# Attention output through DRAM in rows of 448, and a projection of eleven products a tile

## The chip, the cores and the metric

The kernel runs on one core of a Trainium2 chip. The metric is the device time of one execution in microseconds (us); the kernel before has a median of 1062.87 us over three runs (1061.26 to 1063.69). A core has five engines that work side by side, each through its own instructions in their order: TensorE (PE, products of matrices into the banks of PSUM), VectorE (DVE), ScalarE (ACT), GpSimd (POOL) and SyncE (SP), which here only issues DMA transfers.

## The reference

The input x has 2048 rows of 448. Two branches are computed from it and mixed with a gate:

```
g = sigmoid(sum(x * gate_w))
a = attention(x) @ wo        # 16 heads of 28, softmax over 2048 keys
b = gelu(layernorm(x) @ w1 + b1) @ w2 + b2
out = g * a + (1 - g) * b
```

Attention has q, k and v from one matrix of 448 x 1344; scores are q k' / sqrt(28), and each head's output of 28 columns is put beside the others to 448 columns, ahead of wo (448 x 448). All arithmetic is in fp32 accuracy.

## The kernel before

PE multiplies operands in the type float32r, which keeps fewer bits than fp32. So each fp32 operand is split into a rounded high part and a rest, and a product of two operands takes three products of PE: high x high, high x low, low x high.

The stages in order of time: q, k and v are computed and kept in DRAM (0 to about 130 us); the MLP branch runs, and beside it the row maxima of the scores (to about 530 us); its result, with b2 added, is stored in DRAM as `gbs`, 16 tiles of 128 rows. Then comes attention (to about 1020 us), and last the projection with wo and the mix with the gate.

Attention goes over batches `n` from 0 to 15: a group `g` of four heads (`n // 4`) and a chunk `c` of 512 queries (`n % 4`). Each batch has 16 rounds over 128 keys. A round makes twelve products for scores (`scores`, L585), two exponentials on ACT (L594, L598) and four products with v (`value_round`, L762), which add up in bank 7. The four heads stand in partitions 0, 32, 64 and 96 there: 28 rows of output, then one row with the sum of the exponentials (v has a column of ones), then three unused rows.

At the end of a batch `finish` copies bank 7 to `ob` on DVE (L740), POOL's queue takes the four rows of sums to a small tile `lt` (L741), DVE inverts them (L745), POOL's queue writes them to DRAM (`rls`, L746) and brings them back spread over 32 partitions a head (`rc`, L748), and POOL multiplies `ob` by `rc` and splits it into `oh[g][c]` and `ol[g][c]` (L752 to L754). These 32 tiles stay in SBUF, with their unused rows.

The projection (`project`, L768) has 16 tiles of 128 queries, four a chunk. A tile multiplies, for each of the four groups, the high output with the high and the low wo and the low output with the high wo: twelve products (L777) into one of six banks. ACT scales the tile's base `ga`, which was loaded from `gbs`, by 1 - g (L779), DVE adds g times the product (L782), and SP stores the sum to the output (L784). There are six base tiles; the load for tile `tt + 6` (L786) goes into the base that the store of tile `tt` has emptied.

The order is written out by hand: the instructions of each engine run as the program issues them. A planner's clock (`Clock`) advances by a fixed time for each product or round that is issued, and `clock.at(dt, fn)` issues what `fn` holds once that clock has passed `dt` more; `flush` issues all that is left. These due times set only the order: on the chip, an engine works through its list as fast as its waits allow. SP's list holds in attention the loads of q, k and v for later batches (L130, L691) and the small transfers of the row maxima (L302), in the projection the output stores and base loads. `split_q` and `split_k` (L312 to L322) split q and k on POOL.

The projection's tile 0 stands ahead of the last two value rounds, tiles 1 to 11 follow them, then comes `clock.flush()`, then tiles 12 to 15, which need the last chunk.

Of the kernel before, what the change touches and what calls it, by code (L numbers as in the profile page):

```python
# [8 lines left out]
F32 = mybir.dt.float32  # L9
F32R = mybir.dt.float32r  # L10
# [6 lines left out]
P = 128  # L17
S = 2048
D = 448
H = 16  # L20
DH = 28
F = 1792
NG = 4
CH = 512
NC = S // CH
# [46 lines left out]
def kernel(ctx: ExitStack, tc: tile.TileContext, xt, wqk, wv, wo, xk, w1, b1, w2, b2,  # L72
                          ident_d, sel_d, out):
    nc = tc.nc
    ctx.enter_context(tc.manual_schedule())
    clock = Clock()

    const = ctx.enter_context(tc.tile_pool(name="const", bufs=1))
    dram = ctx.enter_context(tc.tile_pool(name="dram", bufs=1, space=DRAM))
# [25 lines left out]
    lns = dram.tile([2 * NT, P], F32, name="lns")  # L105
    gbs = dram.tile([NT, P, D], F32, name="gbs")
    rls = dram.tile([NG * NC, 4, CH], F32, name="rls")

    kr = [kq.tile([P, S], F32R, name=f"kr{i}") for i in range(2)]
    qr = [kq.tile([P, CH], F32R, name=f"qr{i}") for i in range(4)]  # L110
# [13 lines left out]
    def bank(b, n=CH):  # L124
        return ps[:, b, :n]
# [298 lines left out]
    with tc.tile_pool(name="qx", bufs=1) as qx:  # L424
# [105 lines left out]
        at = 3.8  # L530
# [56 lines left out]
    def scores(u):  # L587
        n, k = batches[u]
        a = 3 * (u % 2)
        for which in range(3):  # L590
            for j in range(4):
                product(n, k, j, a + j if j < 3 else 6, which)
        held[u] = z = pz[u % len(pz)]
        nc.scalar.activation(z, bank(6), AF.Exp, scale=SCALE)  # L594

    def exponentials(u):
        a, z, t = 3 * (u % 2), held[u], pt[u % len(pt)]
        nc.scalar.activation(t, ps[:, a:a + 3], AF.Exp, scale=SCALE)  # L598
        held[u] = [t[:, 0], t[:, 1], t[:, 2], z]

    def gates():
        nc.scalar.activation(gate, zall, AF.Exp, scale=-1.0)
        nc.vector.tensor_scalar_add(gate, gate, 1.0)
        nc.vector.reciprocal(gate, gate)
        nc.vector.tensor_scalar(ngate, gate, -1.0, 1.0, op0=OP.mult, op1=OP.add)
# [96 lines left out]
    at = att.enter_context(tc.tile_pool(name="at", bufs=1, reuse_waits="tile"))  # L702
    pt += [at.tile([P, 3, CH], F32, name=f"pt{i}") for i in range(1, 5)]
    pz += [at.tile([P, CH], F32, name=f"pz{i}") for i in range(2, 5)]
    oh = [[at.tile([P, CH], F32R, name=f"oh{g}_{c}") for c in range(NC)] for g in range(NG)]
    ol = [[at.tile([P, CH], F32R, name=f"ol{g}_{c}") for c in range(NC)] for g in range(NG)]
    woh = at.tile([P, NG, D], F32R, name="woh")
    wol = at.tile([P, NG, D], F32R, name="wol")
    ob = at.tile([P, CH], F32, name="ob")
    rc = at.tile([P, CH], F32, name="rc")  # L710
    lt = at.tile([P, CH // 32], F32, name="lt")
    ga = [at.tile([P, D], F32, name=f"ga{i}") for i in range(4)]
    flat = mx.rearrange("p g j t k -> p (g j t k)")
    ga += [flat[:, i * D:i * D + D] for i in range(2)]

    def load_wo(g):
        r = ga[g]
        nc.sync.dma_start(r, wo[:, g])
        clock.at(6.0, split_wo, g, r)

    def split_wo(g, r):
        nc.gpsimd.tensor_copy(woh[:, g], r)
        nc.gpsimd.tensor_sub(wol[:, g], r, woh[:, g].bitcast(F32))

    def load_qr(n):
        g, c = divmod(n, NC)
# [9 lines left out]
        load_heads(k, D, g, slice(0, S))  # L736

    def finish(n):
        g, c = divmod(n, NC)
        nc.vector.tensor_copy(ob, bank(7))  # L740
        nc.gpsimd.dma_start(lt, ob[DH:P:32, :])  # L741
        clock.at(4.0, finish_sum, n, g, c)

    def finish_sum(n, g, c):
        nc.vector.reciprocal(lt, lt)  # L745
        nc.gpsimd.dma_start(rls[n].rearrange("j (a b) -> (j a) b", b=CH // 32), lt)  # L746
        for j in range(4):
            nc.gpsimd.dma_start(rc[32 * j:32 * j + 32], rls[n, j].partition_broadcast(32))  # L748
        clock.at(8.0, finish_split, g, c)

    def finish_split(g, c):
        nc.gpsimd.tensor_mul(ob, ob, rc)  # L752
        nc.gpsimd.tensor_copy(oh[g][c], ob)
        nc.gpsimd.tensor_sub(ol[g][c], ob, oh[g][c].bitcast(F32))  # L754

    def value_round():
        u = state["round"]
        state["round"] += 1
        n, k = batches[u]
        t = held.pop(u)  # L760
        for j in range(4):
            nc.tensor.matmul(ps[32 * j:32 * j + 32, 7], vg[n // NC % 2][:, k, 32 * j:32 * j + 32],  # L762
                             t[j], start=(k == 0), stop=(k == NT - 1),
                             skip_group_check=True)
        if k == NT - 1:
            finish(n)

    def project(tt, b):  # L768
        c, i = divmod(tt, TPC)
        sl = slice(i * P, (i + 1) * P)  # L770
        g = ga[tt % 6]
        ops = []
        for h in range(NG):
            o, l = oh[h][c][:, sl], ol[h][c][:, sl]
            ops += [(o, woh[:, h]), (o, wol[:, h]), (l, woh[:, h])]
        for k, (w, x) in enumerate(ops):
            nc.tensor.matmul(bank(b, D), w, x, start=(k == 0), stop=(k == len(ops) - 1))  # L777
            clock.tick(MN)
        nc.scalar.activation(g, g, AF.Copy, scale=ngate[:, tt:tt + 1])  # L779
        halves = [(nc.sync, slice(0, D))] if tt < NT - 1 else [(nc.sync, slice(0, D // 2)), (nc.scalar, slice(D // 2, D))]  # L780
        for queue, s in halves:
            nc.vector.scalar_tensor_tensor(g[:, s], ps[:, b, s], gate[:, tt:tt + 1], g[:, s],  # L782
                                           op0=OP.mult, op1=OP.add)
            queue.dma_start(out[tt][:, s], g[:, s])  # L784
        if tt + 6 < NT:
            clock.at(4.0, lambda: nc.sync.dma_start(g, gbs[tt + 6]))  # L786

    for u, (n, k) in enumerate(batches):
        if k == 0:
            g, c = divmod(n, NC)  # L790
            if n > 0 and n + 3 < NG * NC:
                clock.at(3.0, load_qr, n + 3)
            if n + 2 < NG * NC:
                clock.at(1.0, split_q, n + 2)
            if c == 1 and g + 1 < NG:
                if g > 0:
                    clock.at(0.0, load_kr, g + 1)
                clock.at(8.0, load_v, g + 1)
            if c == 3 and g + 1 < NG:
                clock.at(2.0, split_k, g + 1)  # L800
            if n == 2:
                for h in range(NG):
                    load_wo(h)
            if n == 14:
                for tt in range(6):
                    nc.sync.dma_start(ga[tt], gbs[tt])
        if u > 1:
            scores(u)
        if u > 0:
            exponentials(u)  # L810
        if u == 8:
            gates()
        clock.tick(0.98)
        if u >= 2:
            value_round()
        clock.tick(0.87)
    project(0, 0)
    value_round()
    value_round()
    for tt in range(1, 12):  # L820
        project(tt, tt % 6)
    clock.flush()
    for tt in range(12, NT):
        project(tt, tt % 6)
    att.close()
# [53 lines left out]
```

## Time and profile before

| | us |
|---|---|
| median of three runs | 1062.87 |
| the profiled execution | 1064.28 |
| its span, first to last instruction | 1062.4 |
| PE busy | 1054.6 (99%) |
| ACT busy | 878.1 (83%) |
| DVE busy | 425.4 (40%) |
| POOL busy | 397.8 (37%) |
| first product of the projection | 1017.34 |
| share of the projection's line in the chain that ended last | 4% |

A row of the timelines reads: start, duration, engine, line, operation, what it writes and reads with shapes, how many were merged, and in brackets how long the engine sat idle before it and what ended that. A name followed by q (SPq) is an engine's issuing of a transfer. A row of the windows reads: the stretch, its length, then the busy time of PE, the weight loads, DVE, ACT and POOL with counts, the granted clock of TensorE as a share of full speed, the busy share of the DMA engines and GB/s. A row of the groups reads: line, engine, operation, shapes, count, then the busy time and the mean ns of one, then idle time before them with its releasers. A row of the chain reads: start, length, engine, line, count. Durations of products overlap, since they are pipelined; the distance of their starts is what counts.

### The profile page before, as it was taken

Reading aid. Unit: us, or ns where it says so; the run is one execution under the profiler, and the core shown is the slowest. Engines: PE = TensorE matmul, PEld = TensorE weight load, DVE = VectorE, ACT = ScalarE, POOL = GpSimd, SP = SyncE. Lnnn points to the kernel's source line nnn. Section 1 sums busy time; section 2 is a strip of 40 time slices with the busy share of each in tenths; the row PEclk is TensorE's granted clock in tenths of the full one; section 3 lists DMA queues with packets and bytes.
Section 4 is the critical chain, followed back from the end, with each engine's and each line's share of the span. In section 5 each row is a group of like instructions: output and inputs, shape, how many; then the busy total and the mean of one; then the engine's idle time right before and its main releaser. Section 6 shows DMA issues by size and latency. Waiting matters only on the chain.

```text
span 1062.4 us, 21453 instructions
## 1 busy us (share of the span) xinstructions
PE 1054.6 (99%) x8120; PEld 583.2 (55%) x8120; DVE 425.4 (40%) x1172; ACT 878.1 (83%) x1239; POOL 397.8 (37%) x410
## 2 busy tenths in 40 slices
PE   8999999999999999999999999999999999999998
PEld 6766766776677677766833333333333333333367
DVE  5488877887788778777300000000000000000012
ACT  5587789877875876686399999999999999999951
POOL 4354737652362336234213552323433242222211
PEclk9999999999999999999999999999999999999999
DMA  8798876513540551241003000300012002000024
GB/s 260 236 301 275 298 263 230 171 49 117 168 133 32 170 171 38 79 140 50 19 10 96 21 21 11 95 20 18 16 39 76 21 11 73 12 12 12 12 82 156
DMA packets 59088, 106.63 MB, mean 100 GB/s; under 512 B 11864, under 2 KB 31576, under 8 KB 58424
## 3 DMA queue, kind: packets, MB, share of 16 engines
q1 hardware_dynamic: 52696, 91.84, 27.8%
q0 software_dynamic: 5856, 12.78, 4.0%
q8 instruction: 64, 1.05, 0.4%
q10 hardware_dynamic: 432, 0.64, 0.2%
q14 instruction: 40, 0.33, 0.1%
HBM read 77.51 MB, written 26.64 MB: 98 GB/s over the span
## 4 chain that ended last, share of the span: by engine, by line
PE 97%; DMA 1%; ACT 1%; DVE 0%; issue 0%; POOL 0%; DVEq 0%; ACTq 0%
PE ps L336 38%; PE ps L762 24%; PE ps L585 22%; PE ps L176 6%; PE ps L777 4%; PE ps L171 4%; DMA kr<-qc 1%; DMA xraw<-in_xt 0%; POOL kr L505 0%; DVE wl L458 0%; ACT rl L258 0%; DVE xl L470 0%; ACT L688 0%; DVE rl L266 0%; ACT hf L328 0%
## 5 line engine op out<-in xcount | busy, mean ns | idle before, releaser
L258 ACT ACTIVATE rl<-ps 128x512 f32<-128x512 f32 x444 | 233.1, 598 | 81.8 <-PE ps L171 57.6
L598 ACT ACTIVATE pt<-ps 128x1536 f32<-128x1536 f32 x204 | 295.4, 1448 | 0.0
L266 DVE CUSTOM_DVE_ANT_0 rl<-rl,ps 128x512 f32<-128x512 f32 x444 | 280.7, 681 | 12.9 <-ACT rl L258 12.5
L762 PE MATMUL ps<-pz,vg 128*32 128x512 f32 x512 | 267.5, 605 | 0.0
L762 PE MATMUL ps<-pt,vg 128*32 128x512 f32 x1224 | 216.1, 605 | 0.0
L585 PEld LDWEIGHTS ps<-qh,kh 29*128 29x128 f32 x1024 | 49.3, 182 | 212.9 <-ACT pz L594 201.1
L740 DVE COPY ob<-ps 128x512 f32<-128x512 f32 x16 | 11.1, 692 | 383.4 <-PE ps L762 383.4
L594 ACT ACTIVATE pz<-ps 128x512 f32<-128x512 f32 x256 | 153.0, 598 | 7.9 <-PE ps L585 7.2
L336 PE MATMUL ps<-yh,w1t 128*128 128x512 f32 x448 | 136.6, 405 | 0.0
L181 DVE TENSOR_REDUCE mx<-ps 128x1 f32<-128x512 f32 x136 | 93.3, 688 | 96.5 <-PE ps L171 55.1
L585 PE MATMUL ps<-qh,kh 29*128 29x512 f32 x1024 | 129.9, 496 | 0.0
L637 POOL TENSOR_TENSOR hl<-hf,hh 128x512 fp32r<-128x512 f32 x56 | 72.2, 1289 | 118.2 <-ACT hh L328 114.9
L171 PE MATMUL ps<-kr,qr 28*128 28x512 f32 x570 | 104.1, 423 | 0.6 <-ACT zall L328 0.5
L585 PE MATMUL ps<-qr,kh 28*128 28x512 f32 x1024 | 104.5, 394 | 0.0
L585 PE MATMUL ps<-qh,kr 28*128 28x512 f32 x1024 | 104.1, 391 | 0.0
L336 PEld LDWEIGHTS ps<-yh,w1t 128*128 128x128 f32 x448 | 80.1, 188 | 33.5 <-issue 19.0
L336 PE MATMUL ps<-w2l,hh 128*128 128x448 f32 x224 | 85.0, 379 | 0.0
L336 PE MATMUL ps<-w2h,hl 128*128 128x448 f32 x224 | 84.7, 378 | 0.0
L336 PE MATMUL ps<-w2h,hh 128*128 128x448 f32 x224 | 84.2, 376 | 0.0
L176 PE MATMUL ps<-kd,qr 28*128 28x512 f32 x444 | 76.5, 497 | 0.0
L598 ACT ACTIVATE rl<-ps 128x1536 f32<-128x1536 f32 x52 | 75.3, 1448 | 0.0
L762 PEld LDWEIGHTS ps<-pt,vg 128*32 128x32 f32 x1224 | 30.8, 108 | 75.5 <-issue 70.6
(125 smaller groups left out, 1487.8 us busy)
## 6 DMA issues: line engine op xcount, KB each, us to landing
w1t<-w1s SPq DMA_DIRECT2D x56, 512.0 KB
qk<-qc SPq DMA_DIRECT2D x28, 256.0 KB
w1s<-w1t POOLq DMA_DIRECT2D x14, 512.0 KB, 5.2
qr<-qk SPq DMA_DIRECT2D x112, 56.0 KB
xr<-in_xt SPq DMA_DIRECT2D x18, 256.0 KB
kr<-qk SPq DMA_DIRECT2D x20, 224.0 KB
vs<-xraw SPq DMA_DIRECT2D x16, 256.0 KB
vg<-vs SPq DMA_DIRECT2D x4, 1024.0 KB
```

Source lines behind the costliest of these rows:

```text
L171: nc.tensor.matmul(bank(b), qr[self.qbuf[g, c]][r, i * P:(i + 1) * P], k[r, kb * CH:(kb + 1) * CH], start=True, stop=True)
L176: nc.tensor.matmul(bank(b), qr[self.qbuf[g, c]][r, i * P:(i + 1) * P], kd[g % 2][r, p], start=True, stop=True)
L181: nc.vector.reduce_max(mx[:, g, j:j + 1, c * TPC + i, kb], ps[:, b:b + 1], axis=AX)
L258: nc.scalar.activation(rl[:, b], bank(1 + b), AF.Relu)
L266: nc.vector.tensor_tensor_reduce(rl[:, b], rl[:, b], bank(k), 1.0, LOW, op0=OP.add, op1=OP.max, accum_out=mx[:, g, j, c * TPC + i, 2 * p:2 ...
L336: nc.tensor.matmul(bank(b, n), w, x, start=(i == 0), stop=(i == len(ops) - 1))
L585: nc.tensor.matmul(bank(b), w, x, start=(which == 0), stop=(which == 2))
L594: nc.scalar.activation(z, bank(6), AF.Exp, scale=SCALE)
L598: nc.scalar.activation(t, ps[:, a:a + 3], AF.Exp, scale=SCALE)
L637: nc.gpsimd.tensor_sub(hl[f], h, hh[f].bitcast(F32))
L762: nc.tensor.matmul(ps[32 * j:32 * j + 32, 7], vg[n // NC % 2][:, k, 32 * j:32 * j + 32], t[j], start=(k == 0), stop=(k == NT - 1), skip_gr ...
L777: nc.tensor.matmul(bank(b, D), w, x, start=(k == 0), stop=(k == len(ops) - 1))
```

## The change

The output of attention goes to a DRAM tensor `od` of 448 x 2048, without the unused rows, and is loaded back by chunks of 512 queries into four blocks of 128 partitions. 448 rows are three and a half blocks: the last 64 rows are loaded twice, into both halves of the fourth block, whose upper half then becomes the low part. So the fourth block needs two products in place of three, and a tile has 3 x 3 + 2 = 11. `wo` is loaded in the same order of rows, its last 64 rows twice, in 22 pieces.

The operands of a chunk are split by three DVE instructions (`split_o`): a copy of 128 x 2048, a subtraction of 128 x 1536 and one of 64 x 512. Two chunks' worth of tiles are kept, so a chunk takes the tiles of the one two before. Chunks 0 and 1 are loaded and split during the last two batches; chunk 2 is loaded after the last value round and split after tile 3; chunk 3 is loaded once its last group is stored, and split after tile 11.

The transfers of `lt`, `rls` and `rc`, which POOL's queue issued, are issued by SP, and so are the four stores to `od` of each batch. POOL keeps the multiplication alone. The due times of the last batch are shorter (2.5 and 5.0 in place of 4.0 and 8.0).

```diff
+    od = dram.tile([D, S], F32, name="od")
...
-    oh = [[at.tile([P, CH], F32R, name=f"oh{g}_{c}") for c in range(NC)] for g in range(NG)]
-    ol = [[at.tile([P, CH], F32R, name=f"ol{g}_{c}") for c in range(NC)] for g in range(NG)]
+    oraw = [at.tile([P, 4, CH], F32, name=f"oraw{i}") for i in range(2)]
+    oh = [at.tile([P, 4, CH], F32R, name=f"oh{i}") for i in range(2)]
+    ol = [at.tile([P, 3, CH], F32R, name=f"ol{i}") for i in range(2)]
...
+    def load_wo():
+        for h in range(H):
+            g, j = divmod(h, 4)
+            a, e = h * DH, h * DH + DH
+            cuts = [a] + [x for x in (P, 2 * P, 3 * P) if a < x < e] + [e]
+            for a, e in zip(cuts, cuts[1:]):
+                r = 32 * j + a - h * DH
+                for p in (a % P,) if a < 3 * P else (a % P, a % P + 64):
+                    nc.sync.dma_start(oraw[1][p:p + e - a, a // P, :D], wo[r:r + e - a, g])
+        clock.at(14.0, split_wo, 0)
...
+    def load_o(c):
+        cs, r = slice(c * CH, (c + 1) * CH), oraw[c % 2]
+        nc.sync.dma_start(r[:, 0:3], od[0:3 * P, cs].rearrange("(t p) n -> p t n", p=P))
+        for p in (0, 64):
+            nc.sync.dma_start(r[p:p + 64, 3], od[3 * P:D, cs])
+
+    def split_o(c):
+        r, h = oraw[c % 2], oh[c % 2]
+        nc.vector.tensor_copy(h, r)
+        nc.vector.tensor_sub(ol[c % 2], r[:, 0:3], h[:, 0:3].bitcast(F32))
+        nc.vector.tensor_sub(h[64:128, 3], r[64:128, 3], h[64:128, 3].bitcast(F32))
...
     def finish(n):
-        g, c = divmod(n, NC)
+        quick = n == NG * NC - 1
         nc.vector.tensor_copy(ob, bank(7))
-        nc.gpsimd.dma_start(lt, ob[DH:P:32, :])
-        clock.at(4.0, finish_sum, n, g, c)
+        nc.sync.dma_start(lt, ob[DH:P:32, :])
+        clock.at(2.5 if quick else 4.0, finish_sum, n, 5.0 if quick else 8.0)
+
+    def finish_sum(n, wait):
+        nc.vector.reciprocal(lt, lt)
+        nc.sync.dma_start(rls[n].rearrange("j (a b) -> (j a) b", b=CH // 32), lt)
+        for j in range(4):
+            nc.sync.dma_start(rc[32 * j:32 * j + 32], rls[n, j].partition_broadcast(32))
+        clock.at(wait, finish_store, n)
+
+    def finish_store(n):
+        g, c = divmod(n, NC)
+        nc.gpsimd.tensor_mul(ob, ob, rc)
         for j in range(4):
+            r = (4 * g + j) * DH
+            nc.sync.dma_start(od[r:r + DH, c * CH:(c + 1) * CH], ob[32 * j:32 * j + DH])
+        if n == NG * NC - 1:
+            load_o(3)
...
+        for t in range(4):
+            o = oh[c % 2][:, t, sl]
+            ops += [(o, woh[:, t]), (o, wol[:, t])]
+            if t < 3:
+                ops += [(ol[c % 2][:, t, sl], woh[:, t])]
...
+            if n >= 14:
+                clock.at(12.0 if n == 14 else 4.0, load_o, n - 14)
+                clock.at(20.0 if n == 14 else 14.0, split_o, n - 14)
...
     value_round()
     value_round()
+    load_o(2)
     for tt in range(1, 12):
         project(tt, tt % 6)
+        if tt == 3:
+            split_o(2)
     clock.flush()
+    split_o(3)
     for tt in range(12, NT):
         project(tt, tt % 6)
```

More of the change, by code (lines that the diff above doesn't have):

```diff
@@ L704 @@
     pz += [at.tile([P, CH], F32, name=f"pz{i}") for i in range(2, 5)]
-    oh = [[at.tile([P, CH], F32R, name=f"oh{g}_{c}") for c in range(NC)] for g in range(NG)]
-    ol = [[at.tile([P, CH], F32R, name=f"ol{g}_{c}") for c in range(NC)] for g in range(NG)]
-    woh = at.tile([P, NG, D], F32R, name="woh")
-    wol = at.tile([P, NG, D], F32R, name="wol")
+    oraw = [at.tile([P, 4, CH], F32, name=f"oraw{i}") for i in range(2)]
+    oh = [at.tile([P, 4, CH], F32R, name=f"oh{i}") for i in range(2)]
+    ol = [at.tile([P, 3, CH], F32R, name=f"ol{i}") for i in range(2)]
+    woh = at.tile([P, 4, D], F32R, name="woh")
+    wol = at.tile([P, 4, D], F32R, name="wol")
     ob = at.tile([P, CH], F32, name="ob")
@@ L714, with split_wo @@
     ga += [flat[:, i * D:i * D + D] for i in range(2)]
[L716 to L723, printed above, removed]
+    def load_wo():
[8 more added lines that the diff above has]
+        clock.at(14.0, split_wo, 0)
+    def split_wo(t):
+        r = oraw[1][:, t, :D]
+        nc.gpsimd.tensor_copy(woh[:, t], r)
+        nc.gpsimd.tensor_sub(wol[:, t], r, woh[:, t].bitcast(F32))
+        if t < 3:
+            clock.at(4.0, split_wo, t + 1)
+    def load_o(c):
[8 more added lines that the diff above has]
+        nc.vector.tensor_sub(h[64:128, 3], r[64:128, 3], h[64:128, 3].bitcast(F32))
     def load_qr(n):
@@ L738, in finish @@
     def finish(n):
-        g, c = divmod(n, NC)
-        nc.vector.tensor_copy(ob, bank(7))
-        nc.gpsimd.dma_start(lt, ob[DH:P:32, :])
-        clock.at(4.0, finish_sum, n, g, c)
-    def finish_sum(n, g, c):
-        nc.vector.reciprocal(lt, lt)
-        nc.gpsimd.dma_start(rls[n].rearrange("j (a b) -> (j a) b", b=CH // 32), lt)
-        for j in range(4):
[L748 to L754, printed above, removed]
+        quick = n == NG * NC - 1
+        nc.vector.tensor_copy(ob, bank(7))
+        nc.sync.dma_start(lt, ob[DH:P:32, :])
[7 more added lines that the diff above has]
+    def finish_store(n):
+        g, c = divmod(n, NC)
+        nc.gpsimd.tensor_mul(ob, ob, rc)
+        for j in range(4):
+            r = (4 * g + j) * DH
+            nc.sync.dma_start(od[r:r + DH, c * CH:(c + 1) * CH], ob[32 * j:32 * j + DH])
+        if n == NG * NC - 1:
+            load_o(3)
     def value_round():
@@ L772, in project @@
         ops = []
-        for h in range(NG):
-            o, l = oh[h][c][:, sl], ol[h][c][:, sl]
-            ops += [(o, woh[:, h]), (o, wol[:, h]), (l, woh[:, h])]
+        for t in range(4):
+            o = oh[c % 2][:, t, sl]
+            ops += [(o, woh[:, t]), (o, wol[:, t])]
+            if t < 3:
+                ops += [(ol[c % 2][:, t, sl], woh[:, t])]
         for k, (w, x) in enumerate(ops):
@@ L801 @@
             if n == 2:
-                for h in range(NG):
-                    load_wo(h)
+                load_wo()
+            if n >= 14:
+                clock.at(12.0 if n == 14 else 4.0, load_o, n - 14)
+                clock.at(20.0 if n == 14 else 14.0, split_o, n - 14)
             if n == 14:
```

## The prediction

> **What bounds the kernel now.** I read the busy table first, then the windows of the attention stretch, then the chain of work that ended last, and last the timelines of the tail engine by engine.
>
> ```profile
> PE 1054.6 (99%) x8120; PEld 583.2 (55%) x8120; DVE 425.4 (40%) x1172; ACT 878.1 (83%) x1239; POOL 397.8 (37%) x410
> ```
>
> ```profile
> 956.20:982.70 26.50, 26.50 (x284) 9.22 (x280) 0.94 (x2) 26.49 (x28) 6.41 (x9) 1.00 0.05 12
> ```
>
> ```profile
> L594 ACT ACTIVATE pz<-ps 128x512 f32<-128x512 f32 x250 | 149.4, 598 | 0.8 <-ACT pt L598 0.5
> ```
>
> The window row gives, after its length, the busy time of PE, weight load, DVE, ACT and POOL, then the granted clock, the DMA share and GB/s. In attention ACT works 26.49 of 26.50 us and sat idle 0.8 us ahead of 250 of its exponentials; DVE works 0.94 and POOL 6.41. Whatever the change does there is free as long as ACT never waits. The tail is different:
>
> ```profile
> 1017.41 2.67 PE ps L777 x12
> ...
> 1021.93 36.68 PE ps L777 x180
> 1058.61 0.03 issue
> ...
> 1058.70 0.45 DVE ga L782
> ```
>
> The projection is a gapless run of PE products: 36.68 / 180 = 0.2038 us each, 2.445 us a tile of twelve, and the end follows the last one. So a product saved is worth 0.2038 us, and a wait of PE costs its full length.
>
> **The products (L777).** Sixteen go, one a tile: 16 x 0.2038 = 3.26 us, all on the path. A tile now takes 11 x 0.2038 = 2.242 us. That is the whole gain; the rest of the change is what it costs to have the operands ready.
>
> **The attention stretch: taken as nothing.** POOL loses a cast and a subtraction a chunk and three kinds of DMA issue. Two splits on DVE (chunks 0 and 1; about 4.2 us each, priced below) lie in windows where DVE works 0.94 of 26.5 us. On SP the transfer of the sums waits for DVE's copy of bank 7, and behind it stand the next loads of q; before, these went out as soon as PE had released the tile:
>
> ```profile
> 589.15 1.63 SPq L130 DMA_DIRECT2D qr<-qk x4
> ```
>
> ```profile
> 619.94 0.61 POOL L312 CAST qh<-qr 128x512 fp32r<-128x512 f32 x1 [7.81 <-PE ps L585]
> ```
>
> A load going out at 589 is wanted by POOL's split no earlier than 620, so a delay of the five or six us by which the copy trails the start of a chunk is covered. Without that cover, each would hold ACT by what is missing. The output stores wait for POOL's multiplication, and behind them again stand only prefetches; the 22 pieces of wo (four before) have from chunk 2 to 1017. If a split stood ahead of the copy of bank 7, PE could wait 4.2 us at most; the splits are called 8 us or more away from it.
>
> **The tail, step by step.** Tile 0 is shorter by one product, so what follows moves 0.20 us ahead: tile 1 starts at 1021.66, tile k ends at 1021.66 + 2.242 k, that is tile 3 at 1028.4 and tile 11 at 1046.3. Tiles 12 to 15 read chunk 3, split by three DVE instructions that the program issues behind tile 11's. DVE takes its instructions in order:
>
> ```profile
> 1021.86 0.47 PE L777 MATMUL ps<-woh,oh 128*128 128x448 f32 x1
> ...
> 1048.51 0.36 PE L777 MATMUL ps<-woh,ol 128*128 128x448 f32 x1
> 1048.71 0.36 PE L777 MATMUL ps<-woh,oh 128*128 128x448 f32 x1
> ```
>
> ```profile
> 1022.06 0.69 DVE L740 COPY ob<-ps 128x512 f32<-128x512 f32 x1 [1.18 <-PE ps L762]
> 1024.64 0.68 DVE L782 SCALAR_TENSOR_TENSOR ga<-ps,gate,ga 128x448 f32<-128x448 f32 x1 [1.89 <-PE ps L777]
> 1028.70 0.25 DVE L745 RECIPROCAL lt<-lt 128x16 f32<-128x16 f32 x1 [3.37 <-DMA lt<-ob]
> 1028.87 1.33 DVE L782 SCALAR_TENSOR_TENSOR ga<-ps,gate,ga 128x448 f32<-128x448 f32 x2
> ...
> 1048.98 0.68 DVE L782 SCALAR_TENSOR_TENSOR mx<-ps,gate,mx 128x448 f32<-128x448 f32 x1 [1.75 <-PE ps L777]
> ```
>
> Tile 2 was through at 1021.86 + 2 x 2.445 = 1026.75, yet its sum ran at 1028.87, because the reciprocal ahead of it waited. So the split can't pass tile 11's sum, and that can't start before 0.27 us past tile 11 (1048.71 to 1048.98). Even with every transfer early, the split starts at 1046.3 + 0.27 + 0.68 = 1047.3, with PE idle since 1046.3.
>
> What the split costs, from DVE rows grouped by shape:
>
> ```profile
> L782 DVE SCALAR_TENSOR_TENSOR ga<-ps,gate,ga 128x448 f32<-128x448 f32 x11 | 7.5, 678 | 40.1 <-ACT ga L779 25.9 <-PE ps L777 14.1
> ...
> L470 DVE TENSOR_TENSOR xl<-xraw,xh 128x512 fp32r<-128x512 f32 x8 | 5.4, 689 | 4.5 <-ACT xh L328 4.5
> ...
> L121 DVE MEMSET kr<- 128x2048 f32 x1 | 1.8, 1765 | 0.4 <-issue 0.4
> ...
> L782 DVE SCALAR_TENSOR_TENSOR ga<-ps,gate,ga 128x224 f32<-128x224 f32 x2 | 0.8, 447 | 1.7 <-PE ps L777 1.7
> ```
>
> Slope (678 - 447) / 224 = 1.03 ns an element. Subtraction of 1536: 0.689 + 1024 x 1.03 ns = 1.74 us. No row shows a copy of 128x2048 on DVE: the memset of that shape took 1.77, the 0.69 copy extended at the slope gives 0.69 + 1536 x 1.03 ns = 2.27. I take 1.77, the row of the same engine and shape, and keep 2.27 for the range. Tile 12's first two products need only the copy; its third needs the long subtraction, which comes 1.74 - 0.41 = 1.3 us after they are done. The last subtraction (0.69) is over before tile 12 reaches its fourth block. So the split alone costs PE 0.95 (sum) + 1.77 + 0.15 (hand-over, an estimate from the 0.27 above) + 1.3 = 4.2 us.
>
> The Trainium skill, VectorE: DVE Perf Modes, section Mode 2×_2P, says that a copy with source and destination both in SBUF can run two fp32 elements a cycle, which would make this copy 1.2 us by an estimate and the sum 0.6 lower; no row here shows such a copy.
>
> **Whether the transfers are in time.** Prices:
>
> ```profile
> 684.21 0.46 SPq L691 DMA_DIRECT2D vg<-vs x1
> ```
>
> ```profile
> 686.00:687.00 1.00, 1.00 (x18) 0.28 (x12) 0.48 (x1) 1.00 (x2) 0.22 (x1) 1.00 0.95 281
> ...
> 689.00:690.00 1.00, 1.00 (x16) 0.50 (x12) 0.00 (x0) 1.00 (x2) 0.00 (x0) 1.00 0.32 68
> ```
>
> ```profile
> 1036.00:1037.00 1.00, 1.00 (x7) 0.93 (x6) 0.18 (x1) 0.44 (x1) 0.00 (x0) 1.00 0.80 303
> ```
>
> ```profile
> lt<-ob POOLq DMA_DIRECT2D x16, 8.0 KB, 3.1
> rls<-lt POOLq DMA_DIRECT2D x16, 8.0 KB, 1.7
> ```
>
> ```profile
> 996.57 1.99 POOL L748 DMA_DIRECT2D rc<-rls x4 [1.42 <-DMA rls<-lt]
> 1000.60 1.28 POOL L752 TENSOR_TENSOR ob<-ob,rc 128x512 f32<-128x512 f32 x1 [2.04 <-DMA rc<-rls]
> ...
> 1031.34 1.99 POOL L748 DMA_DIRECT2D rc<-rls x4 [1.52 <-DMA rls<-lt]
> 1037.50 1.29 POOL L752 TENSOR_TENSOR ob<-ob,rc 128x512 f32<-128x512 f32 x1 [4.17 <-DMA rc<-rls]
> ```
>
> ```profile
> 1033.40 0.33 SPq L786 DMA_DIRECT2D ga<-gbs x1
> ...
> 1042.82 0.38 SPq L786 DMA_DIRECT2D ga<-gbs x1
> ```
>
> ```profile
> 1037.87 0.67 ACT L779 ACTIVATE ga<-ga,ngate 128x448 f32<-128x448 f32 x1 [1.43 <-DMA ga<-gbs]
> ...
> 1045.38 0.67 ACT L779 ACTIVATE ga<-ga,ngate 128x448 f32<-128x448 f32 x1 [1.05 <-DMA ga<-gbs]
> ```
>
> A load of 1 MB moved its data until about 689.2, 5.0 us from its issue (load_o, three issues: 5.4). A 224 KB load took 2.56 us in a calm stretch and 4.47 in a crowded one, so a transfer waits for those ahead of it; at the 303 GB/s of a crowded microsecond of the old tail 224 KB hold the path 0.75. Issues cost about 0.35 each. The path of chunk 3:
>
> - DVE's copy ends at 1022.55; the sums' transfer goes at 1022.6 and lands at 1025.7 (3.1). Right behind it on SP is load_o(2), landed at 1028.4; its split follows tile 3's sum and is over by 1034, ahead of tile 8 (1037.3): free.
> - Reciprocal to 1025.95, rls issued at 1026.0. Landing after 1.7 would be 1027.7; behind load_o(2) and store 1 it is 1029.9. SP waits here with the four broadcasts, and behind them load 6, stores 2 and 3, load 7.
> - First broadcast to multiplication: 4.0, so 1033.9; 1.29 to 1035.2; four stores to od, issued by 1036.5, landed at 1038.2 (1.7). load_o(3) waits for that on SP, with load 8 and store 4 behind it; its data are in at 1043.6, still ahead of tile 11's end.
> - What is late next is the base of tiles 8 to 11 (ga). Load 8, store 4, load 9, store 5 follow the megabyte at 0.75 each: store 4 is through at 1045.1, store 5 at 1046.6. Load 11 refills the tile that store 5 empties: 1046.7 + 2.56 = 1049.3, ACT 0.67, DVE 0.68: the split of chunk 3, behind tile 11's sum, starts at 1050.7 in place of 1047.3.
>
> First product of tile 12: 1050.7 + 1.77 + 0.15 = 1052.6; PE has been idle 6.3 us.
>
> By the Trainium skill, DMA: Bandwidth & Descriptors, section Queues, rings and completion order, each engine takes one queue's descriptors in ring order, so moving the sums to the queue that carries megabytes puts 8 KB behind them: that speaks for the 6.3 and against the 2.9 of the first rival.
>
> **The clock** after such a pause:
>
> ```profile
> 492.00:493.00 1.00, 1.00 (x5) 0.90 (x5) 1.00 (x3) 0.15 (x1) 0.55 (x1) 0.89 1.17 326
> 493.00:494.00 1.00, 1.00 (x4) 0.91 (x3) 0.72 (x4) 0.00 (x0) 0.00 (x0) 0.50 1.25 298
> ...
> 496.00:497.00 1.00, 1.00 (x7) 0.79 (x5) 1.00 (x2) 1.00 (x3) 0.00 (x0) 0.90 0.00 0
> ```
>
> The one drop in this trace, after a thin stretch of PE, held half speed for about 3.4 us, which loses half of that: 1.7. A pause of 6.3 us should bring it; bounds 0 and 1.7, I take 1.7.
>
> **Sum:** -3.26 + 6.3 + 1.3 + 1.7 = +6.0 us. The profiled execution took 1064.28 us round a span of 1062.4, 1.4 above the median; the sum is a difference, so I set it on the median: 1062.87 + 6.0 = 1068.9, about **1069.0 us**.
>
> **Rivals.**
> - *The transfers are in time* (the other side). If small transfers pass the large ones and load 11 lands by 1045.9, only DVE's order is left: 0.95 + 1.77 + 0.15 = 2.9 us of idle, + 1.3 - 3.26 = +0.9, 1063.8 us, not told from no change. For it: the old tail, at up to 303 GB/s, had every base in time, and split chunk 3 on POOL right behind the multiplication at 1037.50, long before tile 12 at 1048.71. Against it: 4.47 against 2.56. If the clock still drops, +2.6: 1065.5.
> - *The transfers are worse.* The broadcasts took 6.2 us (1031.34 to 1037.50) in the crowded tail, and loads 4.47: + 2.2 + 1.9, and the copy at 2.27: +10.6, 1073.5 us.
> - *The split does not stand behind tile 11.* If DVE took it early, the 3.26 us remain: 1059.6. Against it stands the reciprocal's row.
>
> **How the numbers follow.** Forecast 0.60; in time 0.24, half with the clock kept; worse 0.12; early split 0.04. Less than 0.2% (2.1 us) can't be told from no change. Faster 0.04; same 0.14, the first rival with the clock kept and a little of its other half; slower 0.82. The range runs from the first rival, 1063.8, to the second, 1073.5.
>
> **What would show it.** Tiles of eleven products at 2.24 us; on DVE the 128x2048 copy behind tile 11's sum, PE idle by about 6 us at tile 12 with DVE as releaser, and a clock of 0.5 behind it; on SP broadcasts waiting for rls, load_o(3) for the stores of od, and ACT's scalings of bases 8 to 11 ending waits on DMA past 1044. Wrong would be a gap at tile 12 under 3.5 us (transfers in time), none, or waits of ACT in attention.

## The result, and the profile after

The changed kernel takes 1070.75 us (median of six runs, 1069.95 to 1072.54) against 1062.69 before on the same chip, 8.06 us more; the ratio is 1.0083, with a 95% interval of 1.0073 to 1.0093. 1069.0 had been predicted, in a range of 1063.8 to 1073.5.

The profiled execution after took 1070.4 us, that of before 1064.28. The one of before was slower than its six timed runs: its projection began at 1017.34, that of after at 1014.23, and its half clock at 492 to 497 us, which the prediction quotes, has no counterpart after. So the two tails are compared by their length, from the projection's first product to the end of the span: 1062.4 - 1017.34 = 45.06 us before, 1068.4 - 1014.23 = 54.17 after. The tail is 9.11 us longer, and the rest of the kernel is not slower.

PE in the tail, from the timeline of the kernel after (start, duration, what; in brackets the idle time before and its releaser):

```profile
1042.96 0.37 PE L806 MATMUL ps<-wol,oh 128*128 128x448 f32 x1
1051.85 0.74 PE L806 MATMUL ps<-woh,oh 128*128 128x448 f32 x1 [8.52 <-DVE oh L744]
1052.38 0.57 PE L806 MATMUL ps<-wol,oh 128*128 128x448 f32 x1
1053.64 0.74 PE L806 MATMUL ps<-woh,ol 128*128 128x448 f32 x1 [0.68 <-DVE ol L745]
...
1058.27 0.36 PE L806 MATMUL ps<-woh,oh 128*128 128x448 f32 x1
```

Tile 11's last product starts at 1042.96. The next could start 0.20 later; tile 12 starts at 1051.85, released by the copy of the split (L744). Its third product waits once more, for the long subtraction (L745). From there to 1058.27 are twelve steps at 0.386 us in place of 0.204.

What DVE did before that copy, from its timeline:

```profile
1036.06 0.68 DVE L811 SCALAR_TENSOR_TENSOR ga<-ps,gate,ga 128x448 f32<-128x448 f32 x1 [1.34 <-ACT ga L808]
1044.43 0.68 DVE L811 SCALAR_TENSOR_TENSOR ga<-ps,gate,ga 128x448 f32<-128x448 f32 x1 [7.69 <-ACT ga L808]
...
1049.97 0.69 DVE L811 SCALAR_TENSOR_TENSOR mx<-ps,gate,mx 128x448 f32<-128x448 f32 x1 [1.49 <-ACT mx L808]
1050.57 1.22 DVE L744 CAST oh<-oraw 128x2048 fp32r<-128x2048 f32 x1
1051.83 1.76 DVE L745 TENSOR_TENSOR ol<-oraw,oh 128x1536 fp32r<-128x1536 f32 x1
1053.62 0.69 DVE L746 TENSOR_TENSOR oh<-oraw,oh 64x512 fp32r<-64x512 f32 x1
```

The sum of tile 8 waited 7.69 us for ACT's scaling of its base and tile 11's ran at 1049.97; the split of chunk 3 stood behind it. Why the bases were late is on SP:

```profile
1022.46 0.43 SPq L769 DMA_DIRECT2D rls<-lt  x1
1028.57 1.71 SPq L771 DMA_DIRECT2D rc<-rls  x4
...
1033.64 1.61 SPq L779 DMA_DIRECT2D od<-ob  x4
1036.69 0.39 SPq L738 DMA_DIRECT2D oraw<-od  x1
...
1045.42 0.32 SPq L815 DMA_DIRECT2D mx<-gbs  x1
```

```profile
1049.27 0.67 ACT L808 ACTIVATE mx<-mx,ngate 128x448 f32<-128x448 f32 x1 [1.50 <-DMA mx<-gbs]
```

The 8 KB of the sums went out at 1022.46, and the broadcasts that wait for them at 1028.57: 6.1 us. The stores to od, load_o(3) and the base loads follow one after another; load 11 goes out at 1045.42 and ACT has it at 1049.27. In a calm stretch of attention the same pair on SP needs 1.55 us:

```profile
564.60 0.40 SPq L769 DMA_DIRECT2D rls<-lt  x1
566.15 1.71 SPq L771 DMA_DIRECT2D rc<-rls  x4
```

The clock, from the windows of PE in the kernel after (stretch, length, PE busy, granted clock, DMA share, GB/s):

```profile
1044.00:1048.00 4.00, 0.00 (x0) 1.00 0.72 187
1048.00:1052.00 4.00, 0.15 (x1) 0.50 0.82 220
1052.00:1058.00 6.00, 5.32 (x14) 0.50 0.78 220
1058.00:1064.00 6.00, 6.00 (x31) 0.98 0.22 84
```

Half speed held from about 1048 to 1058, six of those ten microseconds with PE at work.

Attention is as it was. The window that the prediction showed of before, and the group of the smaller exponentials, now of after:

```profile
956.20:982.70 26.50, 26.50 (x280) 9.07 (x276) 4.62 (x5) 26.50 (x29) 1.28 (x1) 1.00 0.21 60
```

```profile
L595 ACT ACTIVATE pz<-ps 128x512 f32<-128x512 f32 x251 | 150.1, 598 | 0.6 <-ACT pt L599 0.5
```

ACT works 26.50 of 26.50 us and waited 0.6 us in 251 exponentials; DVE's 4.62 us hold the split of chunk 0, POOL is down from 6.41 to 1.28. So the 9.11 us are all in the tail, and its terms add up to them within 0.1:

| term | predicted, us | profile after, us | from |
|---|---|---|---|
| sixteen products fewer | -3.26 | -3.26 | 0.2038 each |
| gap ahead of tile 12 | +6.3 | +8.7 | 1051.85 - (1042.96 + 0.20) |
| third product's wait | +1.3 | +1.4 | 1053.64 - (1051.85 + 2 x 0.2038) |
| half clock | +1.7 | +2.2 | 1058.27 - 1053.64 - 12 x 0.2038 |
| sum | +6.0 | +9.0 | tail: +9.11 |

### The profile page after: what moved, and what is told of

The parts are those of the page before. It is cut to its first block, busy times and chain, and to the rows that moved or that the text cites. A ratio compares the mean times of both kernels' runs of the same rounds, so it can differ in the third digit from the quotient of the medians.

```text
span 1068.4 us, 21596 instructions
## 1 busy us (share of the span) xinstructions
PE 1053.4 (99%) x8104; PEld 581.0 (54%) x8104; DVE 440.1 (41%) x1184; ACT 878.5 (82%) x1239; POOL 316.1 (30%) x282
## 4 chain that ended last, share of the span: by engine, by line
PE 92%; DMA 4%; DVE 1%; ACT 1%; SPq 1%; issue 1%; POOL 1%; POOLq 0%; DVEq 0%; ACTq 0%
PE ps L337 36%; PE ps L789 24%; PE ps L586 22%; PE ps L177 6%; PE ps L172 3%; PE ps L806 1%; DMA xr<-in_xt 1%; DMA xraw<-in_xt 1%; DMA wraw<-in_wqk 1%; DMA rls<-lt 1%; DMA out_y<-mx 1%; DMA mx<-gbs 0%; DMA r<-in_w 0%; DMA od<-ob 0%; DVE rl L267 0%
## 5 line engine op out<-in xcount | busy, mean ns | idle before, releaser
L267 DVE CUSTOM_DVE_ANT_0 rl<-rl,ps 128x512 f32<-128x512 f32 x444 | 280.8, 682 | 12.5 <-ACT rl L259 12.1
L776 POOL TENSOR_TENSOR ob<-ob,rc 128x512 f32<-128x512 f32 x16 | 20.6, 1288 | 236.4 <-DMA rc<-rls 236.4
```

What stands on the lines that cost most here:

```text
L267: nc.vector.tensor_tensor_reduce(rl[:, b], rl[:, b], bank(k), 1.0, LOW, op0=OP.add, op1=OP.max, accum_out=mx[:, g, j, c * TPC + i, 2 * p:2 ...
```

## The experiments

All are the changed kernel with the edit shown, but for the old kernel with eleven products. The times of the kernel before beside them were 1062.1 to 1062.15 us.

**The gain alone.** The kernel before, with the product of the last group's low output left out in each tile; the term is missing from the output.

```diff
+        ops.pop()
         for k, (w, x) in enumerate(ops):
```

> The kernel before with the twelfth product of each tile left out (low output of the last group times high wo): the gain alone, without the way through DRAM. Theory: sixteen products at 0.2038 us, 1062.7 - 3.26 = 1059.4. Rival (sums, scalings or transfers hold a tile at 2.44 us whatever PE does): less than 1.5 us gained.

Measured: 1058.88 us, ratio 0.9966 (0.9953 to 0.9979), 3.2 less than before. The gain is there in full; the change gives back 12 us elsewhere.

**The order on DVE alone.**

```diff
         if tt == 3:
             split_o(2)
+        if tt == 7:
+            split_o(3)
     clock.flush()
-    split_o(3)
```

> The split of chunk 3 is issued on DVE behind tile 7's sum in place of tile 11's; transfers stay as they are. Theory (the idle of 8.5 us at tile 12 comes from DVE's order, the sums of tiles 8 to 11 standing ahead of the split and waiting for late bases): load_o(3) goes out at 1036.7 and lands about 1043, the copy of 1.22 us is over by about 1044.5 against tile 11's end at 1043.3, so PE idles 1.2 to 1.5 us for the copy and 1.3 for the subtraction, the clock stays at 1.0, and the time is 1062.7 - 3.26 + 2.7 = about 1062, between 1060.5 and 1063.5. Rival (chunk 3 itself comes late through DRAM, the bases are beside the point): the idle stays above 5 us and the time above 1067.

Measured: 1066.12 us, ratio 1.0039 (1.0025 to 1.0053): outside both expectations. PE did about what the theory says; the end did not follow it. Two rows of PE, the copy on DVE, and the end of the chain that ended last:

```profile
1046.87 0.47 PE L806 MATMUL ps<-woh,oh 128*128 128x448 f32 x1 [1.75 <-DVE oh L744]
...
1057.08 0.36 PE L806 MATMUL ps<-wol,oh 128*128 128x448 f32 x1
```

```profile
1045.59 1.23 DVE L744 CAST oh<-oraw 128x2048 fp32r<-128x2048 f32 x1 [6.88 <-DMA oraw<-od]
```

```profile
1052.54 4.04 DMA out_y<-ga
...
1056.59 4.43 DMA ga<-gbs
1061.02 0.02 issue
1061.04 0.68 ACT ga L808
1061.72 0.02 issue
1061.74 0.45 DVE ga L811
```

The gap is 1.75 us: the copy now waits for chunk 3's own load. The last product starts at 1057.08, 41.1 us after the projection's first (1016.02); before it was 40.9 (1058.23 - 1017.34). PE is thus level with the old kernel, but the last sum waits until 1061.74 for base 15, some 4.2 us beyond the 0.47 that it followed the last product by before. A chain of store, load, store, load through six base tiles, each trip about 4 us, has become the bound. So the late bases hold the split in the change, and once the split no longer waits for them they hold the end.

**All bases loaded early, the order on DVE kept.**

```diff
-    ga = [at.tile([P, D], F32, name=f"ga{i}") for i in range(4)]
+    ga = [at.tile([P, D], F32, name=f"ga{i}") for i in range(14)]
...
-        g = ga[tt % 6]
+        g = ga[tt]
...
-        if tt + 6 < NT:
-            clock.at(4.0, lambda: nc.sync.dma_start(g, gbs[tt + 6]))
...
-                for tt in range(6):
+                for tt in range(NT):
```

> All sixteen bases have a tile of their own and are loaded at the start of batch 14, so no base load and no wait for one is left in the tail; the split still stands behind tile 11's sum. Theory (late bases make 5 to 6 us of the idle): the split starts 0.95 us past tile 11, the copy takes 1.22, PE idles about 2.3 us and then 1.3 for the subtraction; with the clock kept 1062.7 - 3.26 + 3.6 = 1063.0, with the clock lost 1065.5. Rival (chunk 3's own path, stores to od and load_o(3), is what comes late): the idle hardly changes, 1068 to 1071.

Measured: 1063.46 us, ratio 1.0018 (1.0007 to 1.0029), 7.3 less than the change. DVE, PE and PE's windows of this kernel:

```profile
1042.90 0.68 DVE L811 SCALAR_TENSOR_TENSOR ga<-ps,gate,ga 128x448 f32<-128x448 f32 x1 [1.55 <-PE ps L806]
1043.51 1.22 DVE L744 CAST oh<-oraw 128x2048 fp32r<-128x2048 f32 x1
```

```profile
1044.78 0.47 PE L806 MATMUL ps<-woh,oh 128*128 128x448 f32 x1 [1.98 <-DVE oh L744]
...
1046.57 0.74 PE L806 MATMUL ps<-woh,ol 128*128 128x448 f32 x1 [1.11 <-DVE ol L745]
```

```profile
1046.00:1050.00 4.00, 3.43 (x10) 0.57 0.00 0
```

Tile 11's sum now waits for PE alone, the split follows at once, and the gap is 1.98 us: the floor that DVE's order sets. Chunk 3's own path was in time. The 6.5 us between 8.52 and 1.98 were the bases, their waits and their traffic together.

**load_o(2) early.**

```diff
+            if n == 15:
+                clock.at(18.0, load_o, 2)
...
-    load_o(2)
```

> load_o(2) is issued 18 us into batch 15, before the last sums, so no megabyte stands ahead of the sums' transfers; all else as changed. Theory (rls took 6.1 us from issue to landing because a megabyte was queued ahead of its 8 KB): rls lands in about 2 us, broadcasts, multiplication, stores and load_o(3) come about 4 us earlier, and so do the bases behind them; the idle falls from 8.5 to about 4.5 us, 1066 to 1067.5. Rival (SP's in-order waits or the write to DRAM itself take the 6 us): rls stays above 5 us and the time within 1 us of 1070.7.

Measured: 1066.9 us, ratio 1.0046 (1.003 to 1.0062). The same pair on SP in this kernel:

```profile
1021.93 1.28 SPq L769 DMA_DIRECT2D rls<-lt  x1
1024.44 1.72 SPq L771 DMA_DIRECT2D rc<-rls  x4
```

```profile
1047.60 0.47 PE L806 MATMUL ps<-woh,oh 128*128 128x448 f32 x1 [4.59 <-DVE oh L744]
```

2.5 us in place of 6.1, and the gap at tile 12 is 4.59 in place of 8.52. The megabyte ahead of the sums is worth the difference; whether by its place in SP's queue or by the load on the DMA engines, this run can't tell.

**The sums' transfers back on POOL's queue.**

```diff
-        nc.sync.dma_start(lt, ob[DH:P:32, :])
+        nc.gpsimd.dma_start(lt, ob[DH:P:32, :])
...
```

and the same for rls and rc.

> The transfers of lt, rls and rc are issued by POOL's queue again, as in the kernel before; everything else as changed, load_o(2) included. Theory (rls is late because it shares SP's queue with a megabyte): rls lands in 2 to 3 us, the multiplication comes 3 to 4 us earlier in spite of POOL's slower issues, and the idle falls by about as much, 1066.5 to 1068. Rival (the DMA engines themselves are full of the megabyte, so no queue helps): rls still takes over 5 us, 1070 to 1071.

Measured: 1070.92 us, ratio 1.0085 (1.0071 to 1.0099), as the change. The expected gain didn't come; POOL's timeline:

```profile
1022.88 0.72 POOL L764 DMA_DIRECT2D lt<-ob  x1 [23.09 <-DVE ga L811]
1027.25 0.55 POOL L769 DMA_DIRECT2D rls<-lt  x1 [3.65 <-DVE lt L768]
1029.57 1.98 POOL L771 DMA_DIRECT2D rc<-rls  x4 [1.76 <-DMA rls<-lt]
1033.68 1.29 POOL L776 TENSOR_TENSOR ob<-ob,rc 128x512 f32<-128x512 f32 x1 [2.14 <-DMA rc<-rls]
```

rls takes 2.3 us here, but the transfer of lt goes out only at 1022.88, 3.2 us after DVE's copy had ended (1018.96 + 0.69), and lands 3.8 later. The multiplication is no earlier for it. The old kernel shows the same late start of lt in its tail, while in attention lt goes out within 0.3 us of the copy. The bracket of lt's row names DVE's sum of tile 1, over at 1022.05 (1021.37 + 0.68), as what ended POOL's wait, and the old kernel's row in its tail names the same sum; whether POOL truly waits for it is not shown. Nor does this run tell the queue's order from the load: the megabyte had gone out at 1018.3 and was through before rls started.

**PE kept busy in the change's gap.**

```diff
     split_o(3)
+    for _ in range(36):
+        nc.tensor.matmul(bank(6, D), woh[:, 0, :P], woh[:, 0], start=True, stop=True)
```

> Between tile 11 and tile 12 PE makes 36 idle products of the same size into the free bank 6 (about 7.3 us of the 8.5 it otherwise sits idle), with nothing else changed. Theory (the pause costs a second time, since the clock stands at half speed until 1058): the clock stays at 1.0, tile 12 starts when it did, and the tail loses the 2.3 us of the half clock: 1068.0 to 1068.8. Rival (the clock would be lost anyway, or costs under 0.5 us): 1070 to 1071.

Measured: 1071.81 us, ratio 1.0093 (1.0075 to 1.0112). No gain. In the profiled execution (1075.01 us, the slowest of the four) the idle products did not reach the end of the gap: base 11 came later there, and tile 12 started 11.4 us after tile 11's end in place of 8.7.

```profile
1055.82 0.48 PE L806 MATMUL ps<-woh,oh 128*128 128x448 f32 x1 [3.89 <-DVE oh L744]
```

```profile
1057.00:1064.00 7.00, 6.39 (x18) 0.52 0.51 160
```

3.89 us stayed idle, and half speed came after it all the same. This run decides nothing on the clock's price. It was tried again where the gap is short and steady.

**PE kept busy in the short gap.** All bases early, as above, and ten idle products behind the split.

```diff
-        g = ga[tt % 6]
+        g = ga[tt]
...
     split_o(3)
+    for _ in range(10):
+        nc.tensor.matmul(bank(6, D), woh[:, 0, :P], woh[:, 0], start=True, stop=True)
```

> The kernel with all sixteen bases loaded early and the split behind tile 11's sum (1063.5 us, pauses of 2.0 and 1.1 us at tile 12, half clock for 2.9 us in its profile), and in addition ten idle products into the free bank 6 between tile 11 and tile 12, 2.04 us, which fill the first pause and leave tile 12's start where it was. Theory (the pause costs a second time through the clock): the clock stays at 1.0 and the time falls by the 1.2 us that the pauses leave unexplained: 1062.1 - 3.26 + 2.0 + 1.4 = 1062.2, 1061.7 to 1062.7. Rival (the clock is lost for another reason, such as the second pause): 1063.5 or more.

Measured: 1061.99 us, ratio 1.0003 (0.9994 to 1.0011), 1.5 below the kernel with all bases (1063.46). Tile 12's first product follows the idle ones without a gap; only the wait of the third is left:

```profile
1046.20 0.47 PE L806 MATMUL ps<-woh,ol 128*128 128x448 f32 x1 [1.12 <-DVE ol L745]
```

```profile
1046.00:1047.00 1.00, 0.80 (x4) 1.00 0.00 0
...
1049.00:1050.00 1.00, 1.00 (x7) 1.00 0.03 13
```

The clock stays at full speed where the kernel with all bases lost it, and the sum without a clock term, 1062.1 - 3.26 + 2.0 + 1.4 = 1062.2, is met within 0.3 us. The half clock is a price of its own: the 1.5 us are half of the 3 us (1046.57 to about 1049.5) that PE worked at half speed in the kernel with all bases.

**All bases and load_o(2) early, the order on DVE kept.** The two edits above together, the base tiles as there.

```diff
-        g = ga[tt % 6]
+        g = ga[tt]
...
+            if n == 15:
+                clock.at(18.0, load_o, 2)
...
-    load_o(2)
```

> All sixteen bases loaded at batch 14 and load_o(2) early, but the split of chunk 3 behind tile 11's sum as in the change. Theory (with every transfer early, DVE's order alone makes the gap): idle of 2.4 and 1.5 us at tile 12 as with the bases alone, 1063 to 1064. Rival (the order doesn't matter once operands are early): no gap, 1058.9.

Measured: 1065.0 us, ratio 1.0025 (1.0012 to 1.0039), 1 to 2 us above the expectation. The gap is that of the kernel with all bases, to 0.01 us; the clock is not:

```profile
1045.50 0.47 PE L806 MATMUL ps<-woh,oh 128*128 128x448 f32 x1 [1.98 <-DVE oh L744]
```

```profile
1046.00:1053.00 7.00, 5.88 (x16) 0.51 0.04 17
```

With every transfer early, DVE's order alone makes the gap, as expected. But after the same pauses half speed held 6.8 us here, 3.4 with the bases alone.

**All bases early and the split behind tile 7.**

```diff
-        g = ga[tt % 6]
+        g = ga[tt]
...
+        if tt == 7:
+            split_o(3)
...
-    split_o(3)
```

> All sixteen bases early and the split of chunk 3 behind tile 7's sum, with load_o(2) where the change has it, ahead of the sums. Theory (then only chunk 3's own lateness through the 6.1 us of rls is left): load_o(3) goes out at about 1035.3 on the axis of the profile with all bases early, where tile 11 ends at 1042.8; it lands after some 6 us, the copy is over by about 1042.5, PE waits at most 0.5 us for it and 1.0 to 1.4 for the subtraction, 1059.0 to 1060.8. Rival (moving the split makes nothing better unless load_o(2) goes out early too): a pause over 2 us, 1062 or more.

Measured: 1059.77 us, ratio 0.9982 (0.9973 to 0.9991), within the expectation: no gap at tile 12, 1.00 us at its third product.

```profile
1044.24 0.47 PE L806 MATMUL ps<-woh,ol 128*128 128x448 f32 x1 [1.00 <-DVE ol L745]
```

**All three edits.**

```diff
-        g = ga[tt % 6]
+        g = ga[tt]
...
+            if n == 15:
+                clock.at(18.0, load_o, 2)
...
-    load_o(2)
...
+        if tt == 7:
+            split_o(3)
...
-    split_o(3)
```

> Three edits together: the split of chunk 3 behind tile 7's sum, all sixteen bases loaded at batch 14, load_o(2) issued in batch 15. Theory (DVE's order, late bases and the megabyte ahead of the sums are the whole loss): load_o(3) lands about 1038, the split is over by about 1041.5, ahead of tile 11's end at 1043, PE never waits and the clock holds; what is left is the gain of sixteen products, 1062.1 - 3.26 = 1058.9, the time of the old kernel with eleven products. Rival (the way through DRAM costs something of its own): a gap at tile 12 or waits in attention, 1061 or more.

Measured: 1058.63 us, ratio 0.9968 (0.9957 to 0.9979), 3.5 us below before and 12.1 below the change. From its chain of waits, and from DVE's timeline:

```profile
1018.67 33.64 PE ps L806 x165
```

```profile
1038.51 1.23 DVE L744 CAST oh<-oraw 128x2048 fp32r<-128x2048 f32 x1 [3.24 <-DMA oraw<-od]
```

The 165 products of tiles 1 to 15 run without a break, and the split is over before tile 11 is. It has the time of the old kernel with eleven products (1058.88), so the way through DRAM costs nothing that can be measured once nothing waits for it.

## Why the prediction was right

**Direction, place and order of events: shown.** The prediction's step that the split stands behind tile 11's sum in DVE's list, and that the sums of tiles 8 to 11 are late because their bases are, is what the profile after shows row by row, and taking either away changes the gap as it should: 8.52 us in the change, 1.98 without late bases, 1.75 with the split moved, none with both.

**The gain** (-3.26): right; -3.2 measured alone.

**Attention as nothing:** right; ACT's wait is 0.6 us in 251 exponentials, with the loads of q behind the sums' transfers.

**The gap (+6.3), mis-sized: 8.7.** Two parts err in opposite directions.

- The copy: 1.77 taken, 1.22 measured. The sentence from the Trainium skill (VectorE: DVE Perf Modes, Mode 2×_2P) gave 1.2 by an estimate, and the trace agrees: 1.22 us for 2048 fp32 elements a partition. A memset, which I took as the nearest row, does not have that rate.
- The split's start: 4.4 us past tile 11's end predicted, 7.4 measured. Moved by the 3.11 us between the two axes (1017.34 - 1014.23), the predicted stations and the measured ones part here:

| station | predicted, on the axis after | measured |
|---|---|---|
| rls issued | 1022.9 | 1022.46 |
| broadcasts go (rls landed) | 1026.8 | 1028.57 |
| load_o(3) goes | 1035.1 | 1036.69 |
| load 11 goes (store 5 through) | 1043.6 | 1045.42 |
| ACT has base 11 | 1046.2 | 1049.27 |
| split of chunk 3 starts | 1047.6 | 1050.57 |

The first 1.8 us go at rls. I let its 8 KB land 0.75 us after load_o(2) and store 1 (1029.9 against 1028.4 + 0.75); the windows show the traffic through at 1026, and the broadcasts went at 1028.57, so the landing of 1.7 us came behind the other transfers and not beside them:

```profile
1025.00:1026.00 1.00, 1.00 (x7) 0.93 (x6) 0.40 (x1) 0.00 (x0) 0.00 (x0) 1.00 0.87 300
1026.00:1027.00 1.00, 1.00 (x7) 0.93 (x6) 0.28 (x1) 0.00 (x0) 0.00 (x0) 1.00 0.08 15
```

The other 1.3 us go at load 11: 2.56 from issue to ACT taken from a calm row, 3.85 measured. A crowded row of before, 4.47, stood beside it and was kept for the range only.

A step that erred without showing in the change is chunk 3's own load. The prediction has its data in at 1043.6, 2.7 us ahead of tile 11's end. With the split moved alone, where the copy waits for that load, it could start only at 1045.59, 0.6 us past tile 11's end (1044.75 + 0.20). In the change the later sums hid this.

**Third product (+1.3):** 1.4, right.

**The clock (+1.7), mis-sized: 2.2.** I took one stretch of 3.4 us; the change has 10 us of half speed, of which PE's pause covers part.

The errors in the gap, the third product and the clock come to 3.0 us in the profile, half of the sum that was predicted. The forecast missed the measured time by only 1.75 us, and that is partly luck: the copy, taken as too slow, offset part of what the transfers were late, and the medians differ by 8.06 us where the tails differ by 9.11. That last 1.05 us is not assigned: the start of the projection alone varies from 1013.33 to 1016.02 between the profiles of the changed kernels.

**The rivals.** *Transfers in time* did not come, but the kernel with all bases is that case: 1063.46 us, 0.3 below its 1063.8 with the clock kept. With the measured copy, 0.55 us faster, that rival gives 1063.3 with the clock kept and 1065.0 with it lost; the clock was lost there for 3.4 us, at a price of 1.5. *Transfers worse* (1073.5) named the right direction of the error. *The split does not stand behind tile 11* is refuted.

**Queue or contention.** Whether the queue's order or the load on the DMA engines delays rls is not shown: the early load_o(2) removes both at once, and the run on POOL's queue came too late to tell the two apart. The rule of the Trainium skill (DMA: Bandwidth & Descriptors, Queues, rings and completion order) that the prediction cites fits the trace, 6.1 us behind a megabyte against 2.5 without it. A hint for it lies in the attention of before, where lt goes out on POOL's queue: from issue to DVE's reciprocal it took 4.43, 3.53 and 3.13 us in three batches with the DMA engines 79 to 88% busy meanwhile, and 2.16 to 3.97 in eleven batches with them at most 13% busy. So full engines alone did not cost that small transfer the 3.6 us that rls lost; but lt is not rls, and the question stays open.

## What to carry to other kernels

An instruction put into an in-order engine's list stands behind the latest wait of everything issued ahead of it: place a step by when its operands are there and by what those ahead of it wait for, here behind tile 7 in place of tile 11. A small transfer on which a chain hangs doesn't belong behind a megabyte, and a ring of buffers refilled by store and load in turn costs a store and a load each, here about 4 us apiece, so spare SBUF is well spent on loading them all at once. Before a saved product is counted, look at who must be ready for the next: eleven products in place of twelve were worth 3.2 us, and a list order, late bases and a late small transfer took 11 us for them.

## What the runs showed of the hardware that was not expected

Short pauses cost the clock, and not always the same. Pauses of 1.98 and 1.11 us, two products between them, brought half speed for 3.4 us in the kernel with all bases (1046.1 to 1049.5) and for 6.8 with load_o(2) early too (1046.2 to 1053.0), though their rows up to there agree to 0.01 us; the change has 10.2 (1048.0 to 1058.2). The drop came 3.5, 2.8 and 4.8 us after PE's pause had begun. Yet pauses of 1.75 and 1.12 us left the clock at full speed:

```profile
1044.00:1050.00 6.00, 3.13 (x15) 1.00 0.76 236
```

That row is of the kernel with the split moved alone, whose pauses lie in its stretch. A single pause of 1.12 us did nothing. The Trainium skill (TensorE: Matmul & The Clock Gate, What's actually happening) has the clock halved after an idle window of about 3.4 us that runs freely and doesn't start with the pause; stretches of 3.4, 6.8 and 10.2 us look like one to three such windows, but pauses that are shorter than a window, with work between them, were enough here.

A copy of 128x2048 from fp32 to fp32r on DVE took 1.22 us, less than the memset of the same shape (1.77).
